# Decode attention with a gated MLP: the V loads issued from ScalarE's queue instead of SyncE's

## Chip, core and metric

The kernel runs on one core of one Trainium2 chip. The metric is the device time of one execution in microseconds (us). The engines are TensorE (PE in the profile), VectorE (DVE), ScalarE (ACT), GpSimd (POOL) and SyncE (SP). SyncE computes nothing here: it issues transfers. The 16 DMA engines of the core move the data between HBM and the on-chip memory (SBUF). Every instruction stream waits and signals through semaphores.

## What is computed

One decoding step for 4 sequences: a layernorm, attention of one query per head over a cache of 8192 positions with 32 heads of size 128, an output projection, a second layernorm and a gated MLP. Cut to what matters:

```python
q = (layernorm(x) @ wq).reshape(B, 1, H, Dh).transpose(0, 2, 1, 3)
scores = einsum("bhqd,bhkd->bhqk", q, k_cache) * Dh ** -0.5
p = softmax(scores)
o = einsum("bhqk,bhkd->bhqd", p, v_cache)
h = x + o.transpose(0, 2, 1, 3).reshape(B, 1, H * Dh) @ wo
n = layernorm(h)
out = h + (sigmoid(n @ w_gate) * (n @ w_up)) @ w_down
```

B = 4, H = 32, Dh = 128, 8192 cached positions, bf16. The two caches are 268 MB each, and each of their bytes is read once. The weights are 14 MB together.

## The kernel before

**Groups and slots.** The work is cut into 32 groups (g = 0 to 31), each of them four heads of one sequence (group g: heads 4(g // 4) to 4(g // 4) + 3 of sequence g % 4). Its K is 8.39 MB (128 partitions, 64 KB to each, one contiguous run of HBM), and its V as much. SBUF has room for three such blocks, the three slots of the tile KV. K(g) lies in slot (2g - 1) % 3 (slot 0 for g = 0), and V(g) is put into the slot that K(g) had (slot 2 for g = 0). K(g + 2) takes the slot of V(g - 1), and so on, so a slot holds K(g), then V(g), then K(g + 3).

**One group.** VectorE transposes K(g) in place in eight pieces (`transpose_k`, L316), after waiting for the load's semaphore. TensorE follows piece by piece with the score matmuls (`scores`, L326, 64 in all). Then `softmax` runs: VectorE finds the maximum and makes the bias (L336 to L341; the token of L341 is `t_a5[g]`, after which K(g) is no longer needed), ScalarE makes the exponentials (L342), VectorE transposes them (L345), ScalarE copies them in four pieces into the tile PT (L349), VectorE works out the reciprocal of the sum (L351 to L355). TensorE then multiplies PT with V (`pv`, L365, 64 matmuls), but one group late: after the scores of g comes P times V of g - 1. VectorE takes its result out (`extract`, L391 to L394, token `t_ox`) one group later again: between the second and the third transpose of K(g) it extracts group g - 2, and waits for that group's `pv` if it must.

**Loads before the change.** All loads are issued by SyncE, in program order, and an instruction that waits holds back those behind it. The order is x, wq, K0, K1, V0, K2, V1, K3, V2, K4 and so on. What each issue waits for: K1 for the transposed x, which is early; V0 for the q projection (`t_qp`, L237), since wq lies in its slot; K2 for `t_a5[0]`; from g = 2 on K(g + 1) for `t_ox[g - 2]`, which tells that V(g - 2) is used up; V(g) for `t_a5[g]`. The last V, V31, goes into slot 0 in three parts (a half and two quarters) once `t_ox[29]` has come. The weights follow, all from SyncE: wo (two parts), w_gate and w_up wait for `t_a5[31]` and go to slot 1, w_down (three parts) waits for the P times V of group 30 and goes to slot 2.

**Where the issues stand in the instruction streams.** `load_v(g)` is called in the main loop behind `softmax(g)` and `fill_q(g + 1)`, and for V31 ahead of `softmax(31)`; `load_v(0)` is called ahead of the loop. `prog.dma(engine, semaphore, ...)` puts the issue at the end of that engine's stream as it stands at the call. The semaphores, the destinations and the waits on data are arguments of the call. ScalarE's stream has, for each group, the exponential (L342), a read of its accumulator and the four copies (L349), and nothing else in the loop.

**The end.** After the scores of group 31 TensorE runs P times V of group 30 (L365), of group 31 (`pv_last`, L379, part by part as V31 lands), the output projection (`project`, L404), the second layernorm's sums, gate and up (L479) and down (L497). The result goes out at L504.

Of the kernel before, what the change touches and what calls it, by code (L numbers as in the profile page):

```python
# [88 lines left out]
def bass_sequential_preLN__mha_block_cached__glu_gated_glu__decode_kernel(  # L89
# [20 lines left out]
    SLOT = 4 * S * DH // 128  # L110
# [5 lines left out]
    prog = _Prog()  # L116
    emit = prog.emit

    with ExitStack() as es:
# [3 lines left out]
        def raw(t):  # L123
            return t.tensor if hasattr(t, "tensor") else t
# [31 lines left out]
        def kv(slot, off, inner, p0=0, np_=128):  # L156
            return bass.AP(raw(KV), p0 * KVROW + slot * SLOT + off, [[KVROW, np_], *inner])
# [10 lines left out]
        for k in keys:  # L168
# [4 lines left out]
        dram_v = lambda g: A_v_cache[g % B, 4 * (g // B):4 * (g // B) + 4, :, :].rearrange(  # L173
            "h (p r) d -> (h p) (r d)", p=32)
# [81 lines left out]
        t_v, t_et, t_pv, t_ox = {}, {}, {}, {}  # L256
# [19 lines left out]
        def load_v(g):  # L276
            last = g == NG - 1
            vslot[g] = slot = 0 if last else (2 * g + 2) % 3
            w = [t_ox[g - 2]] if last else [t_a5[g]] if g else [t_qp]
            if last:  # L280
                t_v[g] = []
                for i, (lo, hi) in enumerate(((0, 2), (2, 3), (3, 4))):
                    q = SLOT // 4
                    t = prog.dma("sp", f"vp{i}", lambda e, lo=lo, hi=hi, q=q: e.dma_start(
                        kv(slot, q * lo, [[1, q * (hi - lo)]]), dram_v(g)[:, q * lo:q * hi]), w)
                    t_v[g] += [t] * (hi - lo)
            else:
                t_v[g] = [prog.dma("sp", f"v{slot}", lambda e: e.dma_start(kv(slot, 0, [[1, SLOT]]), dram_v(g)), w)] * 4

        t_w = {}  # L290
        kslot, vslot = {}, {}
# [119 lines left out]
        load_k(0)  # L411
        load_k(1)
        load_v(0)
        TURNS = (NG - 2) // 3
        assert 2 + 3 * TURNS == NG
        for g in range(NG):
# [11 lines left out]
            if g > 1:  # L428
                keep_o(g - 2)
                if g + 1 < NG:  # L430
                    load_k(g + 1)
                else:
                    load_v(g)
# [3 lines left out]
            if 0 < g < NG - 1:  # L437
                load_v(g)
# [67 lines left out]
        key, v = t_out  # L506
# [55 lines left out]
```

## Time and profile before

| | |
|---|---|
| time, median of 3 runs | 1279.83 us (1279.78 to 1279.93) |
| the profiled execution: its time | 1279.91 us |
| the profiled execution: its span, first to last instruction | 1278.0 us |
| busy: PE, DVE, ACT | 1002.8 us (78%), 698.5 us (55%), 84.5 us (7%) |
| granted TensorE clock, mean | 0.915 |
| read from HBM | 550.77 MB, 431 GB/s over the span |
| issue of a K or V load on SyncE | 0.33 us each |
| K loads: issue to landing, median of 32 | 32.5 us |
| V loads (8.39 MB): issue to landing, median of 31 | 34.3 us |

Times in the profile count from the first instruction. The trace lists instructions, not the travel of each load; where a load's landing matters, it is read from the first instruction that had waited for it, for K(g) the first transpose of its group (L316). The busy times of the engines say little by themselves: an engine that is idle because the data has not come is not the limit.

### The profile page before, as it was taken

The page shows a single profiled execution, that of the slowest core. Times are in us where ns is not written, and L with a number is a line of the kernel's source. Part 1 is how long each engine was busy: PE and PEld are TensorE (multiplying, and loading weights), DVE is VectorE, ACT ScalarE, POOL GpSimd, SP SyncE. Part 2 cuts the span into 40 slices and gives each one's busy share as a digit, 9 for nine tenths or more (in the row PEclk, how much of TensorE's full clock was granted, in tenths as well). Part 3 has the DMA queues.
Part 4 walks back from the last instruction along what each step waited for, and adds up shares of the span by engine and source line. Part 5 has one row for each costly group of instructions (what it writes and reads, how often), then busy time and mean ns, then how long its engine had stood idle before and what let it go on. Part 6 is the DMA issues. An engine that isn't in the chain of part 4 may idle for free. (4 is left out here: it accounts for less than half of the span.)

```text
span 1278.0 us, 11089 instructions
## 1 busy us (share of the span) xinstructions
PE 1002.8 (78%) x4532; PEld 415.2 (32%) x4532; DVE 698.5 (55%) x728; ACT 84.5 (7%) x202; POOL 19.9 (2%) x80
## 2 busy tenths in 40 slices
PE   1598777779777789777788777788777797777798
PEld 1233323333233333223333233333233332333335
DVE  0765665446655446654456654456654456554461
ACT  0000000000000000000000000000000000000010
POOL 1000000000000000000000000000000000000000
PEclk9899888899888898888998888998888998888988
DMA  9999999999999999999999999999999999999998
GB/s 407 445 424 425 435 444 431 427 439 435 437 429 435 431 445 429 427 439 439 435 427 439 435 435 431 435 431 443 431 429 437 439 435 427 439 435 435 429 423 356
DMA packets 11582, 550.96 MB, mean 431 GB/s; under 512 B 1192, under 2 KB 1200, under 8 KB 2736
## 3 DMA queue, kind: packets, MB, share of 16 engines
q1 hardware_dynamic: 11568, 550.78, 99.6%
q8 instruction: 8, 0.13, 0.0%
q14 instruction: 6, 0.05, 0.0%
HBM read 550.77 MB, written 0.00 MB: 431 GB/s over the span
## 5 line engine op out<-in xcount | busy, mean ns | idle before, releaser
L316 DVE STREAM_TRANSPOSE KV<-KV 128x2048 uint32<-128x2048 uint32 x256 | 568.5, 2278 | 381.3 <-DVEq L52 381.3
L326 PE MATMUL PS<-KV,Lq 128*128 128x512 bf16 x2048 | 543.2, 416 | 258.8 <-PEq L52 258.0
L365 PE MATMUL PS<-KV,PT 128*128 128x512 bf16 x1984 | 433.2, 379 | 0.0
L326 PEld LDWEIGHTS PS<-KV,Lq 128*128 128x128 bf16 x2048 | 199.3, 104 | 602.2 <-issue 443.0
L365 PEld LDWEIGHTS PS<-KV,PT 128*128 128x128 bf16 x1984 | 193.9, 98 | 234.5
L342 ACT ACTIVATE E_sb<-PS,TS 128x512 bf16<-128x512 f32 x32 | 22.0, 688 | 1125.0 <-DVE TS L341 1125.0
L336 DVE TENSOR_REDUCE TS<-PS 128x1 f32<-128x512 f32 x32 | 22.1, 691 | 70.4 <-DVEq L52 70.4
L349 ACT ACTIVATE PT<-ET 32x256 bf16<-32x256 bf16 x128 | 53.0, 414 | 30.8 <-DVE ET L345 28.5
L345 DVE STREAM_TRANSPOSE ET<-E_sb 128x512 bf16<-128x512 bf16 x32 | 22.8, 711 | 30.7 <-DVEq L52 30.7
L391 DVE STREAM_TRANSPOSE OX<-PS 128x512 f32<-128x512 f32 x32 | 21.7, 677 | 21.0 <-PE PS L379 12.3
L264 POOL TENSOR_TENSOR Lq<-q_all,mask 128x16 bf16<-128x16 bf16 x32 | 8.4, 263 | 575.6 <-DVE TS L341 563.7
L268 POOL COPY OT<-OTs 128x4 bf16<-128x4 bf16 x30 | 5.8, 192 | 623.1 <-DVE OTs L394 623.1
L379 PE MATMUL PS<-KV,PT 128*128 128x512 bf16 x64 | 14.0, 379 | 0.0
L237 PE MATMUL PS<-xnT,KV 128*128 128x4 bf16 x128 | 3.6, 166 | 9.7 <-DMA KV<-in_A_wq_dram 9.7
L354 DVE STREAM_TRANSPOSE TS<-TS 128x32 f32<-128x32 f32 x32 | 6.8, 212 | 4.7
L341 DVE STREAM_TRANSPOSE TS<-TS 128x32 f32<-128x32 f32 x32 | 6.8, 212 | 4.7
L337 DVE STREAM_TRANSPOSE TS<-TS 128x32 f32<-128x32 f32 x32 | 6.8, 212 | 4.7
L394 DVE TENSOR_SCALAR OTs<-Or,small 128x4 bf16<-128x4 f32 x30 | 6.9, 229 | 4.5 <-DVEq L52 0.5
L379 PEld LDWEIGHTS PS<-KV,PT 128*128 128x128 bf16 x64 | 6.3, 98 | 7.5
L339 DVE TENSOR_SCALAR TS<-small 128x32 f32<-128x32 f32 x32 | 5.8, 181 | 5.0 <-DVEq L52 0.6
L353 DVE COPY TS<-small 128x32 f32<-128x32 f32 x32 | 5.8, 181 | 4.7
L393 DVE TENSOR_REDUCE Or<-OX 128x4 f32<-128x16 f32 x32 | 5.7, 179 | 4.7
(65 smaller groups left out, 75.6 us busy)
## 6 DMA issues: line engine op xcount, KB each, us to landing
KV<-in_A_wq_dram SPq DMA_DIRECT2D x1, 4096.0 KB, 12.2
KV<-in_A_v_cache_dram SPq DMA_DIRECT2D x1, 4096.0 KB, 22.8
KV<-in_A_v_cache_dram SPq DMA_DIRECT2D x2, 2048.0 KB, 29.5
KV<-in_A_wo_dram SPq DMA_DIRECT2D x1, 3072.0 KB, 22.5
KV<-in_B_w_gate_dram SPq DMA_DIRECT2D x1, 1792.0 KB, 28.0
KV<-in_B_w_up_dram SPq DMA_DIRECT2D x1, 1792.0 KB, 23.2
KV<-in_A_wo_dram SPq DMA_DIRECT2D x1, 1024.0 KB, 24.6
KV<-in_B_w_down_dram SPq DMA_DIRECT2D x1, 1024.0 KB, 23.2
```

The costliest lines, as they stand in the source:

```text
L264: emit("pool", lambda e: e.tensor_tensor(dst, src, msk, ALU.mult), [t_q, t_mk, t_lq0, t_a5.get(g - 1), t_oc.get(g - 3)], key="lq")
L316: emit("dve", lambda e: e.transpose(v, v), key="tp", take=take, keep=keep)
L326: ins = e.matmul(S_b[0], Lq[:, hp, 15 - s:15 - s + 128], rhs, start=(s == 0 and hp == 0), stop=(s == NS - 1 and hp == 3))
L336: dv(lambda e: e.tensor_reduce(TS[:, 0, 0:1], S_b[0], AX.X, ALU.max), [t_ts0] if g == 0 else [], [("sc", 1)])
L337: dv(lambda e: e.transpose(TS[:, 1, :], TS[:, 0, :]))
L342: emit("act", lambda e: e.activation(E_sb[:, :], S_b[0], ACT.Exp, bias=TS[:, 3, 0:1], scale=SCALE, accum_out=TS[:, 4, 0:1]), [t_a5[g]], ke ...
L345: t_et[g] = dv(lambda e: e.transpose(ET[:, :], E_sb[:, :]), take=[("ex", 1)], key="dve")
L349: emit("act", lambda e, dst=dst, src=src: e.activation(dst, src, ACT.Copy), [t_et[g], t_pt0], key="pt")
L365: ins = e.matmul(O_b, PT[:, u3, off:off + 128], rhs, start=(j == 0 and rl == 0), stop=(j == 3 and rl == NS - 1))
L379: ins = e.matmul(V_b, PT[:, u3, off:off + 128], rhs, start=(j == 0 and rl == 0), stop=(j == 3 and rl == NS - 1))
L391: emit("dve", lambda e: e.transpose(OX[:, :, :].rearrange("p (r i) x -> p r i x", r=4), src), w, key="dv", take=take, keep=keep)
L394: t_ox[g] = emit("dve", lambda e: e.tensor_scalar(dst, Or[:, :], small[:, 2 + g % 3:3 + g % 3], None, op0=ALU.mult), take=[("dv", 1)], kee ...
```

## The change

`load_v` issues V from ScalarE's queue; K and the weights stay on SyncE's. Destinations, sizes, semaphores and the named waits are as before.

```diff
@@ load_v(g) @@
                 for i, (lo, hi) in enumerate(((0, 2), (2, 3), (3, 4))):
                     q = SLOT // 4
-                    t = prog.dma("sp", f"vp{i}", lambda e, lo=lo, hi=hi, q=q: e.dma_start(
+                    t = prog.dma("act", f"vp{i}", lambda e, lo=lo, hi=hi, q=q: e.dma_start(
                         kv(slot, q * lo, [[1, q * (hi - lo)]]), dram_v(g)[:, q * lo:q * hi]), w)
                     t_v[g] += [t] * (hi - lo)
             else:
-                t_v[g] = [prog.dma("sp", f"v{slot}", lambda e: e.dma_start(kv(slot, 0, [[1, SLOT]]), dram_v(g)), w)] * 4
+                t_v[g] = [prog.dma("act", f"v{slot}", lambda e: e.dma_start(kv(slot, 0, [[1, SLOT]]), dram_v(g)), w)] * 4
```

ScalarE's stream gains 34 issues: V0 behind the layernorm's square root (L212), V(g) for g = 1 to 30 behind the four copies of L349 of the same group, and the three parts of V31 ahead of the exponential of group 31. SyncE's stream loses the same 34. PE's, DVE's and POOL's streams are the same. In ScalarE's stream V(g) needs no wait of its own for `t_a5[g]`, because the exponential ahead of it has waited for that token already.

## The prediction

> **What bounds the kernel now.** I read the DMA rows of the page first, then the busy times by stretch, then SyncE's timeline beside VectorE's.
>
> ```profile
> DMA  9999999999999999999999999999999999999998
> GB/s 407 445 424 425 435 444 431 427 439 435 437 429 435 431 445 429 427 439 439 435 427 439 435 435 431 435 431 443 431 429 437 439 435 427 439 435 435 429 423 356
> DMA packets 11582, 550.96 MB, mean 431 GB/s; under 512 B 1192, under 2 KB 1200, under 8 KB 2736
> q1 hardware_dynamic: 11568, 550.78, 99.6%
> ```
>
> ```profile
> 440.00:640.00 200.00, 159.12 (x650) 64.24 (x651) 114.70 (x116) 12.18 (x30) 2.47 (x11) 0.90 1.00 435
> ```
>
> The DMA engines are never free: 99.6% of the span on one queue, and in the middle a share of 1.00 (the column before the last). So one queue already keeps all 16 engines busy; "two loads under way" has no idle bandwidth to fill. The order of the loads is what can change. How it works in the steady part, from the timeline (start, duration, engine, line):
>
> ```profile
> 600.68 0.33 SPq L274 DMA_DIRECT2D KV<-in_A_k_cache_dram  x1
> ...
> 618.11 0.33 SPq L288 DMA_DIRECT2D KV<-in_A_v_cache_dram  x1
> ...
> 633.43 4.51 DVE L316 STREAM_TRANSPOSE KV<-KV 128x2048 uint32<-128x2048 uint32 x2 [12.27 <-DVEq L52]
> ...
> 639.26 0.33 SPq L274 DMA_DIRECT2D KV<-in_A_k_cache_dram  x1
> ...
> 656.70 0.33 SPq L288 DMA_DIRECT2D KV<-in_A_v_cache_dram  x1
> ...
> 672.11 4.51 DVE L316 STREAM_TRANSPOSE KV<-KV 128x2048 uint32<-128x2048 uint32 x2 [12.37 <-DVEq L52]
> ```
>
> A K lands (L316 starts, 633.43), the next lands 38.7 later; from 131.27 (K3) to 1213.04 (K31) it is 1081.8/28 = 38.63 us for a K and a V, so **19.3 us a load** (8.39 MB, 434 GB/s). 5.84 after a landing the next K is issued (the extract sits behind two transposes), 23.3 after it V (`t_a5`). Each waits 12 to 15 us in the queue behind the load under way: that is why the engines never run dry, and why **a K gets the whole bandwidth while it is under way**.
>
> **The change, part by part.** *The issues.* 34 issues of 0.33 us move to ScalarE, which is busy 7% of the span: nothing. V(g) now stands behind the exponential and the four copies: L342 starts at 81.79, the last L349 ends at 83.45 + 1.73 = 85.18, so V is issued **3.4 us later**, 26.7 after K's landing. In the steady part it used to queue some 15 us, so alone this costs nothing; where the queue is empty it costs 3.4. SyncE loses nothing it needed and gains nothing: no K was held back there by a V's wait (K2 went at its own `t_a5[0]`, 56.33, with V0 gone since 17.04).
>
> *The sharing.* V no longer queues behind K; both are under way together. No row shows two queues at once. Bounds: K all the bandwidth or V all of it. I take equal shares, since the packets are alike (11,582 packets, most of them the 64 KB rows of K and V). A load issued into an empty queue I start 1.4 after its issue (x: issued 0.74, used 2.18). I replay it by hand with these numbers.
>
> *The start.* Rows of before:
>
> ```profile
> 13.43 3.58 PE L237 MATMUL PS<-xnT,KV 128*128 128x4 bf16 x128 [9.67 <-DMA KV<-in_A_wq_dram]
> ...
> 17.04 0.33 SPq L288 DMA_DIRECT2D KV<-in_A_v_cache_dram  x1
> ...
> 34.35 17.66 DVE L316 STREAM_TRANSPOSE KV<-KV 128x2048 uint32<-128x2048 uint32 x8 [16.30 <-DVEq L52]
> ...
> 56.33 0.33 SPq L274 DMA_DIRECT2D KV<-in_A_k_cache_dram  x1
> ...
> 59.58 17.66 DVE L316 STREAM_TRANSPOSE KV<-KV 128x2048 uint32<-128x2048 uint32 x8 [0.20 <-DVEq L52]
> ...
> 79.14 13.97 PE L365 MATMUL PS<-KV,PT 128*128 128x512 bf16 x64
> ...
> 81.78 0.33 SPq L288 DMA_DIRECT2D KV<-in_A_v_cache_dram  x1
> ...
> 92.44 4.50 DVE L316 STREAM_TRANSPOSE KV<-KV 128x2048 uint32<-128x2048 uint32 x2 [7.61 <-DVEq L52]
> ```
>
> Before, K0, K1, V0, K2 land at 34.35, 53.7, 73.1, 92.44. Now V0 (issued 17.04, moving at 18.4) shares with K0, of which 15.9 us are left: K0 lands at 18.4 + 31.9 = 50.3, V0 at 57.2, K1 at 73.1 (the same bytes). `t_a5[0]` is 21.98 after K0 (34.35 to 56.33): 72.3, so K2 starts at 73.7 (hole 0.6) and lands at 93.0. VectorE is free for K1 3.25 later (56.33 to 59.58) at 75.5; `t_a5[1]` 22.2 after (59.58 to 81.78): 97.7; V1 is issued 3.4 later, at 101.1, and moves at 102.5. K3 is no help: it waits for the extract of group 0, and P times V of group 0 ends 11.3 after `t_a5[1]` (79.14 + 13.97 against 81.78), at 109.0, so K3 is issued at 110.4. From 93.0 to 102.5 **nothing is under way: 9.5 us**. With the 0.6: 10.1 lost. The reason is that V0, which nobody needs before 92, now delays K0 and K1, on which all waits hang.
>
> *The middle.* From 102.5: V1 alone to 111.8, where K3 joins; V1's last 10.0 take 20.0, it lands at 131.8. V2 starts at 132.7 (the extract of group 0 holds VectorE's third transpose to 110.3; then 13.3 of transposes, 4.3 from the last of them to `t_a5`, 3.4 and 1.4). In the same way: K3 has 8.4 left, lands at 149.5; K4 starts at 156.7; V2 lands at 164.1; V3 starts at 177.6 (149.5 + 26.7 + 1.4), K4 lands at 181.8, K5 starts at 189.0, V3 lands at 209.0, V4 starts at 209.9, K5 lands at 226.7. K5 is 77.2 after K3, four loads' worth: from there it repeats, odd K slow, even K quick, **and the queue is never empty: 0**.
>
> *The end.* K31 (odd, slow) lands at 149.5 + 14 x 77.26 = 1231.1, against
>
> ```profile
> 1213.04 4.50 DVE L316 STREAM_TRANSPOSE KV<-KV 128x2048 uint32<-128x2048 uint32 x2 [12.37 <-DVEq L52]
> ...
> 1247.72 13.98 PE L379 MATMUL PS<-KV,PT 128*128 128x512 bf16 x64
> ...
> 1261.54 4.41 PE L404 MATMUL PS<-OT,KV 128*128 128x4 bf16 x128
> ```
>
> 18.1 late: the 10.1 of the holes, and 8.0 because V30 has moved ahead of it. From K31's landing to the end before is 1278.0 - 1213.04 = 65.0 us of PE work without a gap: scores to 1234, L365, L379 (each 14), then the chain from L404 on. It goes along: **1231.1 + 65.0 = 1296.1**. The data is no later than this chain: after K31 before, V30, V31 and 9.4 MB of weights move (19.3 + 19.3 + 21.7 = 60.3); now V30 has 8.4 of that behind it, so all has landed by 1231.1 + 51.9 = 1283, and w_down is used 59.7 after K31 (L497, 1272.70), at 1290.8. V31's last quarter is wanted 45 after K31, at 1276; even with equal shares against the weights it is in by 1267.
>
> **Sum.** Span 1278.0 + 10.1 + 8.0 = 1296.1. The profiled execution took 1279.91, 1.9 over its span and 0.08 over the median, so I add 1.9: **1298.0 us, 1.4% slower**. The bounds of the unknown share, K wholly or V wholly first, are worked out among the rivals.
>
> **The rivals.**
> *Whole loads take turns* (a variant with nearly the same answer). V0 runs between K0 and K1; the hole after K2 stays, the middle has the old order, so K31 is some 9.5 late: 1222.6. V31's last quarter then waits for the wo loads in its turns (9.7 us): 1251.6 + 9.5 + 9.7 = 1270.8, and 3.5 + 16.3 (L379's end at 1261.7 to 1278.0) after it: 1290.6, 1292.5 with the 1.9. [...]
>
> *Nothing changes.* If the engines serve the two queues in order of issue, the old order returns: V0 is issued behind K1 (1.6 to 2.8) and ahead of K2, V31 ahead of the weights, and V's 3.4 us are hidden by the 15 of queueing: 1279.9. For it: the bytes are the same and the engines full (99.6%). Against it: each queue can hold its order only for itself. (If SyncE's queue is wholly first, the start's hole closes, but wo, w_gate and w_up, 7.9 MB or 18 us, go ahead of V31, which lands at some 1270 instead of 1251.6: 1270 + 3.5 + 16.3 + 1.9 = 1291.) [...]
>
> *Faster: two queues move more bytes per second.* If the pause between loads is closed, the rate may rise. The highest slice is 445 against 434: 551 MB would take 1238 instead of 1270 us, 31 less, less the 18 above: 1267. It decides from 434 x (1 + 18/1270) = 440 GB/s on. Against it: the share is 1.00 with no pause to see, and slices scatter from 424 to 445 around a steady 19.3 us a load.
>
> *Much slower: V gets the larger share*, or mixed reading lowers the rate. With V at 60% (K3's last 8.4 take 21, V2 moves 12.6 beside it) V2 lands before K4 starts, and a hole opens in each pair of groups; I estimate 2 to 3 us, some third of the 9 below, and in 15 pairs that is 30 to 45: 1330 to 1345. With V wholly first a K gets only what V leaves: of each pair the second K lands 12 late behind V, 7.2 of nothing (5.84 + 1.4) follow and 1.6 at the next V, about 9 us: 1278 + 15 x 9 = 1413, an end too far to take in. A rate lower by 1% adds 12.7: 1311.
>
> **Chances.** Equal shares (with unequal ones in favour of K, 1291) 0.59, whole loads in turn 0.14, no change 0.05, higher rate 0.05, V ahead or lower rate 0.17. The range takes in the first two, some of the lower rate, and reaches down for the start's hole being half as long: 1284 to 1313. This measurement tells about 0.2% from no change. Faster 0.05, same 0.05, slower 0.90.
>
> **What would show it.** Right: V0 issued near 17 on ScalarE; K0's L316 near 50 instead of 34; a slice or two near 90 to 105 with a DMA share under 9; from there 9 throughout at 434 GB/s; landings of K (L316) in turns of about 32 and 45 apart; K31 near 1231, the 65 us after it unchanged. Wrong: K0 at 34 (K first), dry slices all along (V first), a rate other than 434 with the share at 1.00, or an end bound by w_down's landing.

## The result, and the profile after

The changed kernel takes **1298.23 us** (median of 4 runs, 1296.58 to 1298.97) against 1279.80 before (4 runs, 1279.55 to 1279.93): ratio 1.0142, 95% interval 1.0129 to 1.0154. It is slower by 18.4 us. The profiled execution took 1298.97 us with a span of 1297.1.

The first view to compare is the page's DMA part, as before: slices of the span, then the queues.

```profile
DMA  9979999999999999999999999999999999999996
GB/s 417 422 326 421 425 437 433 416 426 445 423 445 428 435 439 424 447 423 445 428 435 439 424 445 424 445 428 435 439 426 443 425 445 428 435 439 422 447 412 253
q1 hardware_dynamic: 6672, 282.34, 50.5%
q10 hardware_dynamic: 4896, 268.44, 47.8%
```

There are two queues now, q1 (SyncE's) and q10 (ScalarE's), but together they fill the engines no better than the one did: 98.3% of a longer span against 99.6%. The third slice has fallen from 424 to 326 GB/s; no other has by so much, but for the last. The same in figures, busy times by stretch (the last two columns are DMA share and GB/s), after:

```profile
90.00:105.00 15.00, 14.71 (x69) 6.48 (x67) 8.10 (x14) 2.43 (x6) 0.26 (x1) 1.00 0.53 211
120.00:240.00 120.00, 89.97 (x365) 35.96 (x363) 59.59 (x64) 7.30 (x18) 1.37 (x6) 0.89 1.00 427
240.00:440.00 200.00, 158.51 (x675) 63.98 (x676) 116.80 (x120) 12.94 (x32) 2.54 (x11) 0.96 1.00 434
440.00:640.00 200.00, 159.92 (x665) 64.46 (x664) 109.71 (x116) 13.57 (x34) 2.27 (x10) 0.92 1.00 434
```

and before:

```profile
120.00:240.00 120.00, 96.54 (x404) 39.27 (x403) 65.06 (x66) 7.30 (x18) 1.37 (x6) 0.91 1.00 435
240.00:440.00 200.00, 158.26 (x656) 63.98 (x654) 108.43 (x110) 12.18 (x30) 2.28 (x10) 0.91 1.00 433
```

From 240 us on the rate is that of before, although K and V loads share the engines in every pair of groups there: **mixing rows of equal size costs nothing there**. The loss sits in the first 240 us, and in something that the rate does not show. The start, from the changed kernel's timeline (start, duration, engine, line):

```profile
17.13 0.37 ACTq L288 DMA_DIRECT2D KV<-in_A_v_cache_dram  x1
...
46.27 17.66 DVE L316 STREAM_TRANSPOSE KV<-KV 128x2048 uint32<-128x2048 uint32 x8 [28.13 <-DVEq L52]
...
72.94 17.66 DVE L316 STREAM_TRANSPOSE KV<-KV 128x2048 uint32<-128x2048 uint32 x8 [1.64 <-DVEq L52]
...
95.14 0.69 ACT L342 ACTIVATE E_sb<-PS,TS 128x512 bf16<-128x512 f32 x1 [23.48 <-DVE TS L341]
...
96.82 0.34 ACTq L288 DMA_DIRECT2D KV<-in_A_v_cache_dram  x1
...
106.61 0.72 DVE L391 STREAM_TRANSPOSE OX<-PS 128x512 f32<-128x512 f32 x1 [3.65 <-DVEq L52]
...
149.34 4.50 DVE L316 STREAM_TRANSPOSE KV<-KV 128x2048 uint32<-128x2048 uint32 x2 [20.80 <-DVEq L52]
```

K0 lands at 46.27 instead of 34.35, K1 some 19 us later than before at 72.9. So V1, whose issue needs the bias of group 1, goes at 96.82 instead of 81.78, when K2 is in and nothing else is under way: by the trace's DMA packets K2's last row ends at 91.5 and V1's first starts at 97.8. K3 cannot help: it waits for the extract of group 0 (L391 at 106.61).

The end, from the same timeline:

```profile
1188.65 4.51 DVE L316 STREAM_TRANSPOSE KV<-KV 128x2048 uint32<-128x2048 uint32 x2 [7.48 <-DVEq L52]
...
1213.60 0.34 ACTq L288 DMA_DIRECT2D KV<-in_A_v_cache_dram  x1
...
1232.11 4.50 DVE L316 STREAM_TRANSPOSE KV<-KV 128x2048 uint32<-128x2048 uint32 x2 [17.15 <-DVEq L52]
...
1266.80 13.98 PE L379 MATMUL PS<-KV,PT 128*128 128x512 bf16 x64
```

K31 lands at 1232.11, 43.5 after K30; V30, issued at 1213.60, travels beside it. From K31's landing to the end are 1297.1 - 1232.11 = 65.0 us, as before. So **the whole loss is K31's 19.07 us of delay**. Adding up the bytes of the trace's DMA packets (a packet under way counted in part) divides it. MB moved by a given time:

| by (us) | before | after | V0 alone on ScalarE's queue | V30, V31 back on SyncE's |
|---|---|---|---|---|
| 120 | 50.66 | 47.09 | 47.42 | 46.61 |
| 240 | 102.71 | 98.03 | 99.41 | 97.65 |
| 1200 | 519.54 | 514.78 | 516.25 | 514.12 |
| K31's landing | 525.2 | 528.7 | 525.3 | 525.4 |

(The two kernels on the right are experiments told below.) After against before: 3.57 MB behind at 120 us, 4.68 at 240, 4.76 at 1200; at 434 GB/s that is 8.2, 10.8 and 11.0 us. By K31's landing 3.5 MB more have moved than before, V30's head start: 8.1 us. 11.0 + 8.1 = 19.1.

### The profile page after: what moved, and what is told of

Same layout as the page of the kernel before. It is cut to its first block, busy times and chain, and to the rows that moved or that the text cites. A ratio compares the mean times of both kernels' runs of the same rounds, so it can differ in the third digit from the quotient of the medians.

```text
span 1297.1 us, 11089 instructions
## 1 busy us (share of the span) xinstructions
PE 996.6 (77%) x4532; PEld 410.8 (32%) x4532; DVE 698.5 (54%) x728; ACT 84.4 (7%) x202; POOL 19.9 (2%) x80
## 5 line engine op out<-in xcount | busy, mean ns | idle before, releaser
L326 PE MATMUL PS<-KV,Lq 128*128 128x512 bf16 x2048 | 518.9, 400 | 234.2 <-PEq L52 233.8
L365 PE MATMUL PS<-KV,PT 128*128 128x512 bf16 x1984 | 449.2, 389 | 49.8 <-PEq L52 49.8
L326 PEld LDWEIGHTS PS<-KV,Lq 128*128 128x128 bf16 x2048 | 191.9, 101 | 560.3 <-issue 388.1
L365 PEld LDWEIGHTS PS<-KV,PT 128*128 128x128 bf16 x1984 | 196.8, 100 | 299.8 <-issue 78.4
L336 DVE TENSOR_REDUCE TS<-PS 128x1 f32<-128x512 f32 x32 | 22.1, 692 | 70.4 <-DVEq L52 70.4
L349 ACT ACTIVATE PT<-ET 32x256 bf16<-32x256 bf16 x128 | 52.9, 413 | 30.8 <-DVE ET L345 28.5
L391 DVE STREAM_TRANSPOSE OX<-PS 128x512 f32<-128x512 f32 x32 | 21.7, 678 | 24.6 <-DVEq L52 12.3
L379 PE MATMUL PS<-KV,PT 128*128 128x512 bf16 x64 | 14.0, 379 | 0.0
L379 PEld LDWEIGHTS PS<-KV,PT 128*128 128x128 bf16 x64 | 6.2, 97 | 7.6
## 6 DMA issues: line engine op xcount, KB each, us to landing
KV<-in_A_wq_dram SPq DMA_DIRECT2D x1, 4096.0 KB, 12.3
```

Of the source, the lines that this page charges most:

```text
L326: ins = e.matmul(S_b[0], Lq[:, hp, 15 - s:15 - s + 128], rhs, start=(s == 0 and hp == 0), stop=(s == NS - 1 and hp == 3))
L336: dv(lambda e: e.tensor_reduce(TS[:, 0, 0:1], S_b[0], AX.X, ALU.max), [t_ts0] if g == 0 else [], [("sc", 1)])
L349: emit("act", lambda e, dst=dst, src=src: e.activation(dst, src, ACT.Copy), [t_et[g], t_pt0], key="pt")
L365: ins = e.matmul(O_b, PT[:, u3, off:off + 128], rhs, start=(j == 0 and rl == 0), stop=(j == 3 and rl == NS - 1))
L379: ins = e.matmul(V_b, PT[:, u3, off:off + 128], rhs, start=(j == 0 and rl == 0), stop=(j == 3 and rl == NS - 1))
L391: emit("dve", lambda e: e.transpose(OX[:, :, :].rearrange("p (r i) x -> p r i x", r=4), src), w, key="dv", take=take, keep=keep)
```

## The experiments

The theory to test: sharing costs nothing by itself; the loss is the *order* of loads in two places, V0 beside K0 and K1 (a hole behind K2), and V30 beside K31 (K31 late, with 65 us of work behind it). The main rival: a price of every V load on ScalarE's queue, or of mixed reading. Unless it says otherwise, an experiment starts from the changed kernel; the kernel before was measured again beside each set (1279.82 us for the first four, 1279.77 for the three with halves), and the ratios are to that; "K31" is the start of its first transposes, and "rest" the span from there to the end.

| kernel | time, us | ratio to before (95%) | K31 | rest |
|---|---|---|---|---|
| before | 1279.82 | | 1213.04 | 65.0 |
| after | 1298.23 | 1.0142 (1.0129 to 1.0154) | 1232.11 | 65.0 |
| V0 on SyncE | 1284.50 | 1.0034 (1.0022 to 1.0047) | 1217.78 | 64.8 |
| V0 alone on ScalarE | 1287.68 | 1.0061 (1.0044 to 1.0077) | 1220.87 | 65.2 |
| V30, V31 on SyncE | 1292.43 | 1.0095 (1.0078 to 1.0111) | 1225.96 | 64.8 |
| V0, V30, V31 on SyncE | 1279.94 | 1.0001 (0.9991 to 1.0010) | 1212.99 | 65.0 |
| K in halves | 1369.47 | 1.0701 (1.0679 to 1.0722) | 1302.30 | 65.1 |
| V in halves | 1306.56 | 1.0210 (1.0169 to 1.0251) | 1231.74 | 72.5 |
| K in halves, one queue | 1281.13 | 1.0010 (1.0000 to 1.0021) | 1214.18 | 65.0 |

**V0 back on SyncE's queue.**

```diff
-t_v[g] = [prog.dma("act", f"v{slot}", ...
+t_v[g] = [prog.dma("act" if g else "sp", f"v{slot}", ...
```

Expected: 

> V0 goes back to SyncE's queue; V1 to V31 stay on ScalarE's. Theory (order): the changed kernel is late because V0 shares with K0 and K1, which opens a hole in the loads after K2, and because V30 overtakes part of K31; sharing as such costs nothing. Then K0 and K1 land as before (34 and 54), the stretch from 90 to 105 us has no hole (DMA share 1.00 there, 0.53 in the changed kernel), K2 becomes the slow one of the pairs, K31 a quick one that V30 overtakes by some 3 us only: K31 lands at 1214 to 1217, span 1280 to 1283, time 1282 to 1285. Rival (a price for each V on ScalarE's queue, or for mixed reading: 19.1 us over 32 V loads, 0.6 us each): time 1297. Second rival (only the first load's wait matters, the end does not): as the order theory at the start, but K31 still late by 8 to 9: time 1288 to 1290.

Measured: 1284.50 us, K31 at 1217.78. The hole is gone; the stretch from 90 to 105 us:

```profile
90.00:105.00 15.00, 8.24 (x29) 3.05 (x27) 7.36 (x6) 0.00 (x0) 0.19 (x1) 0.77 1.05 455
```

31 V loads still go through ScalarE, and three quarters of the loss are gone, so the price per V load falls. One thing was not as expected: K does not alternate between slow and quick here; from 97.34 (K2) on a K lands every 38.6 us. So K31 came 0.8 us behind the expected range, while the time is inside it and under the 1288 to 1290 of the second rival. K31 is 4.7 late: by its landing 527.3 MB have moved, 2.1 more than before, 4.8 us of V30.

**Only V0 on ScalarE's queue** (from the kernel before).

```diff
-t_v[g] = [prog.dma("sp", f"v{slot}", ...
+t_v[g] = [prog.dma("sp" if g else "act", f"v{slot}", ...
```

Expected: 

> Only V0 is issued from ScalarE; V1 to V31 are on SyncE's queue as before. Theory (order): the start's share alone. K0 lands near 46, K1 near 73, and between K2's end and V1, which now has to wait for the bias of group 1, nothing is under way for 6 to 8 us; the rest runs in the old order, with no V ahead of K31. K31 lands at 1219 to 1222, span 1284 to 1287, time 1286 to 1289. Rival (a price for each V on ScalarE's queue): 1280.5. Rival (nothing but the mixing in the middle costs): 1280.

Measured: 1287.68 us, K31 at 1220.87, 7.8 late. One load of K or V on another queue, of 64, costs 0.6%:

```profile
90.00:105.00 15.00, 14.73 (x69) 6.47 (x67) 8.98 (x14) 2.44 (x6) 0.27 (x1) 1.00 0.59 233
...
96.02 0.33 SPq L288 DMA_DIRECT2D KV<-in_A_v_cache_dram  x1
99.35 4.50 DVE L316 STREAM_TRANSPOSE KV<-KV 128x2048 uint32<-128x2048 uint32 x2 [0.28 <-DVEq L52]
```

The first line is of the stretches, the others of the timeline: V1, on SyncE's queue as ever, goes at 96.02 into an empty queue. Both rivals had 1280 to 1280.5.

**V30 and V31 back on SyncE's queue.**

```diff
-t = prog.dma("act", f"vp{i}", ...
+t = prog.dma("sp", f"vp{i}", ...
-t_v[g] = [prog.dma("act", f"v{slot}", ...
+t_v[g] = [prog.dma("act" if g < NG - 2 else "sp", f"v{slot}", ...
```

Expected: 

> V30 and V31 go back to SyncE's queue, behind K31; V0 to V29 stay on ScalarE's. Theory (order): the hole at the start stays (about 10), but nothing overtakes K31 now. K31 lands some 8 us earlier than in the changed kernel, at 1222 to 1225, the 65 us behind it are the same, span 1287 to 1290, time 1289 to 1292. Rival (a price for each V): 1297. Rival (the end is set by the weights' landing, which shares with V31 no more): the span would not follow K31, and the last 65 us would be longer or shorter.

Measured: 1292.43 us, 5.8 less than the changed kernel and 0.4 over the range; K31 at 1225.96, 6.2 earlier and 1 us later than its range. By K31's landing 525.4 MB have moved, as before the change (525.2), so nothing that counts overtakes it; the start cost this kernel more (5.42 MB behind at 1200 us, 12.5 us, against 11.0). The rest is 64.8: the weights' landing does not set the end.

**V0, V30 and V31 on SyncE's queue**, both edits together.

```diff
-t_v[g] = [prog.dma("act", f"v{slot}", ...
+t_v[g] = [prog.dma("act" if 0 < g < NG - 2 else "sp", f"v{slot}", ...
```

Expected: 

> V0, V30 and V31 on SyncE's queue, V1 to V29 on ScalarE's: 29 of 32 V loads still share with K all through the middle. Theory (order): neither hole nor overtaking is left, so the time is that of the kernel before within 0.2%: 1278 to 1282, K31 landing at 1213 to 1215. Rival (a price for each V, or a lower rate of mixed reading): 29/32 of the loss stays, 1296 to 1297.

Measured: 1279.94 us, ratio 1.0001 (0.9991 to 1.0010), and 243 MB on ScalarE's queue:

```profile
q1 hardware_dynamic: 7392, 307.51, 55.7%
q10 hardware_dynamic: 4176, 243.27, 43.9%
```

So 29 of 32 V loads on the second queue cost nothing that can be measured, and bring nothing. The rival (1296 to 1297) falls.

**Each K load in two halves.** Two transfers with rows of 32 KB instead of one with rows of 64 KB, on the same queue; the first transpose waits for both.

```diff
-prog.dma("sp", f"sl{slot}", lambda e: e.dma_start(kv(slot, 0, [[1, SLOT]]), dram_k(g)), w)
+for i in range(2):
+    q = SLOT // 2
+    prog.dma("sp", f"sl{slot}", lambda e, i=i, q=q: e.dma_start(
+        kv(slot, q * i, [[1, q]]), dram_k(g)[:, q * i:q * (i + 1)]), w)
...
-take = [] if i else [(f"sl{slot}", 16), ...
+take = [] if i else [(f"sl{slot}", 32), ...
```

Expected: 

> The changed kernel with each K load cut into two transfers of 32 KB a row (the wait is for both); V's rows stay 64 KB. Tells how the engines share two queues. Theory (turns by packet, one row each): V gets twice K's bytes while both are under way, V lands early and K late, a hole of 5 to 8 us opens in every pair of groups, the DMA share falls under 0.95 all along: time 1370 to 1420. Rival (shares by bytes): as the changed kernel, 1298 within 3. Rival (whole loads in turn): the second half of K waits for a whole V, much as the first.

Measured: 1369.47 us, 0.5 under the theory's range, and far from 1298. A stretch in the middle, and three K landings:

```profile
840.00:1040.00 200.00, 154.90 (x676) 64.20 (x675) 109.69 (x116) 13.82 (x34) 2.28 (x10) 0.91 0.97 417
```

```profile
1058.49 4.50 DVE L319 STREAM_TRANSPOSE KV<-KV 128x2048 uint32<-128x2048 uint32 x2 [24.32 <-DVEq L52]
...
1086.40 4.50 DVE L319 STREAM_TRANSPOSE KV<-KV 128x2048 uint32<-128x2048 uint32 x2 [1.60 <-DVEq L52]
...
1139.73 4.51 DVE L319 STREAM_TRANSPOSE KV<-KV 128x2048 uint32<-128x2048 uint32 x2 [24.32 <-DVEq L52]
```

A pair of groups takes 81.2 us (1058.49 to 1139.73) instead of 77.2. That is 4 us more in each (a hole of 5 to 8 was expected, and a DMA share under 0.95, not 0.97); by the packets an engine moves nothing for 3.0 of these 81.2 us. The hole opens since V is in before the next K may be issued; that V moves twice K's bytes while both travel is an estimate from the rows' sizes, 64 KB against 32. The 14 pairs from K3 to K31 make 58 of the 89.3 us of K31's delay. K3 is 31 us late already (162.22 instead of 131.27): by the start, where the third slice of the page is down to 270 GB/s, and by the V that moves beside it. The bytes and the queues are the same, and so is the order on each queue: only the size of K's transfers and rows has changed, and with it the shares: K0 lands at 53.60 instead of 46.27. So the engines did not share by bytes here.

**The control: K in halves on the one queue of before** (the same edit on the kernel before).

Expected: 

> The control for the two before: the kernel before (one queue) with each K load cut into two transfers of 32 KB a row. One queue has no turns to share. Expected by every theory of sharing: 1280 within 2, since 32 more issues of 0.33 us are hidden. If smaller rows themselves cost, it shows here.

Measured: 1281.13 us, 1.0010 (1.0000 to 1.0021): smaller rows cost about 0.1% here, so the 71 us more than the changed kernel above are the sharing.

**Each V load in two halves** (V0 to V30; K's rows whole).

```diff
-t_v[g] = [prog.dma("act", f"v{slot}", lambda e: e.dma_start(kv(slot, 0, [[1, SLOT]]), dram_v(g)), w)] * 4
+for i in range(2):
+    q = SLOT // 2
+    t = prog.dma("act", f"v{slot}", lambda e, i=i, q=q: e.dma_start(
+        kv(slot, q * i, [[1, q]]), dram_v(g)[:, q * i:q * (i + 1)]), w)
+t_v[g] = [t] * 4
...
-take = [("pt", 4), (f"v{slot}", 16)] if j == 0 else []
+take = [("pt", 4), (f"v{slot}", 32)] if j == 0 else []
```

Expected: 

> The changed kernel with each of V0 to V30 cut into two transfers of 32 KB a row; K's rows stay 64 KB. Theory (turns by packet): K gets twice V's bytes while both are under way. V0 takes less from K0 and K1, the hole after K2 shrinks to some 5 us, V30 overtakes less of K31: time 1288 to 1293, faster than the changed kernel by 5 to 10. Rival (shares by bytes): 1298 within 3.

Measured: 1306.56 us (1300.57 to 1312.34): a miss, slower than the changed kernel (1296.58 to 1298.97) where faster was expected. The start went as expected: K0 lands at 40.16 (46.27 in the changed kernel), and DMA moves 315 GB/s from 90 to 105 us (211). By 240 us this kernel has moved 2.5 MB (5.7 us) more than the changed one. But by 1200 us it is 2.3 MB behind it, so 11 us are lost in the middle, where the kernels with whole rows hold 432 to 435 GB/s. Two stretches of it:

```profile
240.00:440.00 200.00, 152.18 (x655) 62.30 (x653) 113.41 (x122) 14.59 (x36) 2.54 (x11) 0.91 0.99 425
840.00:1040.00 200.00, 160.42 (x699) 66.44 (x697) 111.76 (x113) 12.16 (x30) 2.27 (x10) 0.92 1.00 427
```

The engines are as good as full there, but some rows last longer than the usual 2.42 us (64 KB) and 1.21 us (32 KB), up to 3.5. By the packets that is some 6 of the 11 us; why they do is open. So K31 lands no earlier than in the changed kernel. And at the end V is late. The timeline around K31's landing (L369 is P times V, L395 the extract's first step):

```profile
1227.36 16.29 PE L369 MATMUL PS<-KV,PT 128*128 128x512 bf16 x64 [13.92 <-PEq L52]
1231.74 4.50 DVE L320 STREAM_TRANSPOSE KV<-KV 128x2048 uint32<-128x2048 uint32 x2 [13.01 <-DVEq L52]
1243.48 3.65 PE L330 MATMUL PS<-KV,Lq 128*128 128x512 bf16 x16
1243.80 0.72 DVE L395 STREAM_TRANSPOSE OX<-PS 128x512 f32<-128x512 f32 x1 [7.55 <-DVEq L52]
```

P times V of group 29 starts only at 1227.36, with V29's landing (TensorE had waited 13.92 us for it). K31 is there at 1231.74, and VectorE makes two transposes; then it stands 7.55 us at the extract of group 29, until P times V ends, with six transposes of K31 behind it. The rest is 72.5 instead of 65.0. Over the whole span VectorE waits 120.8 us at this step, where the kernel before has 8.7 and the changed kernel 12.3:

```profile
DVE OX L395 <- DVEq L52: 120.8, 19, 11.6
```

(total, times, longest). So there was a bound on either side: with V's rows of 32 KB against K's 64, V came too late for `extract` (1306.56 us), with K's rows of 32 KB against V's 64, K came too late (1369.47). Equal rows, between the two, took 1298.23. In the profiled execution (1306.01 us, 7.0 over that of the changed kernel) K31 lands within 0.4 us of the changed kernel's, so the 7.5 behind it are the difference. That is read from the trace; no run took the wait away, and the executions of this kernel vary by 12 us.

No version beat both kernels. The bound is the bytes: in the kernel before, the engines are busy for 99.6% of the span, at 433 to 435 GB/s in the middle, and no kernel here moved more there.

## Why the prediction was right

It gave 1298.0 us, and 1298.23 was measured. That it is so close is luck: two errors of 1.9 and 2.6 us at the start nearly cancel, and the median lies 0.7 under the profiled execution, whose span is 1.0 over the forecast. The mechanism is the one that was forecast. By its steps:

- *Sharing in equal parts.* Held. K lands in turns 43.4 and 33.8 us apart (1111.43, 1154.86, 1188.65, 1232.11; 45 and 32 forecast), 77.2 a pair, and cutting one side's rows in halves moved the shares the way turns by row would: K0 lands at 46.27 with equal rows, at 53.60 with K's in halves, at 40.16 with V's in halves. The changed kernel's packets show the turns themselves: from 22 to 41 us they start in rounds of 16, one of V0's queue, then one of K0's, and so on.
- *The hole at the start, 10.1 us.* Measured 8.2 by 120 us and 10.8 by 240. Three sizes in it were off. K0 landed at 46.27, not 50.3, since V0's first rows start at 22.1, 5.0 behind its issue, and not at 18.4; this moved little, as K1's landing (72.94, forecast 73.1) sets the rest. And V is not issued 3.4 us behind its bias but 1.7 (95.14 to 96.82), as the last section tells: V1 went at 96.82, not 101.1. The hole is shorter by that, but between 120 and 240 us the rate is 427 instead of 435 GB/s, and 1.1 MB less are moved: 2.6 us that the forecast had at nothing. Some row transfers in that stretch last up to 4.3 us instead of 2.42, by the packets. Why is not settled. The kernel with V30 and V31 on SyncE, which has the hole and shares behind it, loses 1.0 MB there too. The hole alone does not do it (by the table's bytes, V0 alone on ScalarE loses under 0.1 MB from 120 to 240 us), and sharing equal rows alone does not either (435 GB/s with V0 on SyncE and with all three). V in halves lost some 6 us in this way far behind its hole.
- *The middle, nothing.* Held: 434 GB/s; 29 V loads through ScalarE with no hole and no overtaking gave 1.0001.
- *K31 behind V30, 8.0 us.* Held: 3.5 MB, 8.1 us, in this phase of the pairs. Taking it away brought 6.2 us of K31's landing, since that kernel lost 1.5 us more at its start. The size depends on how V30 and K31 meet: 4.8 us with V0 on SyncE.
- *The 65.0 us behind K31.* Held in eight of nine kernels within 0.2 us; it moved only where VectorE was held in the midst of K31 by the extract.
- *The rivals.* "Nothing changes" names the right thing, that there is no bandwidth to gain, and the wrong result, for the second queue changes which load comes first. The trace has 434 GB/s with one queue and with two. The order of issue did not hold across the queues: K1, issued by 2.8, had its first row at 46.3, and V0, issued at 17.13, at 22.1. The 18 us lie in the order of the loads. "Whole loads take turns" falls with K0: it would have landed at 34 with V0 behind it, and it lands at 46.27. In the changed kernel's trace the packets of 64 KB, 2.42 us each, alternate between q10 and q1 one by one where both queues hold rows (22 to 41 us), so a turn was one row here. "Much slower, V ahead" was no case of the changed kernel but is real: it is the kernel with K in halves, 1369 us, for which the forecast's 1330 to 1345 (V at 60%) and 1413 (V wholly first) are the two sides. The 2 to 3 us a pair behind the first were an estimate that the forecast's own replay does not give: there V at 60% leaves a hole of only 0.5 us (V2 in at 160.4, K4 off at 160.9), and V at two thirds one of 4.7, near the 4 measured. (The sum for SyncE's queue wholly first comes to 1291.7, not 1291.)

## What to carry to other kernels

Here, with the DMA engines full, a second queue added no bandwidth (434 GB/s either way); it took away an order. In a kernel like this one, look for the loads that the first waits and the last stretch of work hang on (here K0, K1 and K31) and keep other loads from travelling beside them; in between, where a load is always queued, sharing rows of equal size cost nothing (1.0001). Where the two queues shared here, the sizes of their rows set the shares (K0 at 40.16, 46.27 or 53.60), and both sides were starved in turn (1369 and 1307 us): check who waits for the slower one before favouring the other.

## What the runs showed of the hardware

- The two queues here took turns by row, not by bytes: in the changed kernel their packets alternate one row each from 22 to 41 us; rows of 64 KB against rows of 64 KB shared about evenly (K0 lands at 46.3 to 48.8 instead of 34.3 beside V0); 32 KB rows of K against 64 KB rows of V cost 71 us more than equal rows, and on one queue the same cut cost 1.4.
- Behind K0's rows the trace has 16 packets of 4 bytes, and K0's first transpose starts 0.7 us behind the last of them (33.65 and 34.35 before, 45.58 and 46.27 after), so they are read as the signals of the landing. They took a turn too: before the change K0's rows end at 31.8 to 33.7 and the signals go at once; in the changed kernel they end at 41.4 to 43.2 and the signals go at 43.9 to 45.6, one row of V0 (2.42 us) later.
- ScalarE issued V1, V2 and V3 while the copies ahead of them in its stream still ran. In the changed kernel V1 goes at 96.82, 0.01 after the first of the four copies that stand ahead of it has started; the last three of them start at 97.25 and take 1.29 us. V2 (127.18 behind 127.17) and V3 (174.29 behind 174.28) are the same. So these issues were held back by the wait that stands before those copies, and not by their work.
